# Batch 2's probabilities turned by a DMA crossing, batch 3's scores ahead of batch 2's packed product, slot 1's stores from GpSimd, packed keys turned at step 14

## The chip, the cores and the metric

The kernel runs on one core of one Trainium2 chip. The metric is the device time of one launch in microseconds, the median of several runs. Engines are named as in the profile: PE (TensorE, matrix products), PEld (its weight loads), ACT (ScalarE), DVE (VectorE), POOL (GpSimd) and SP (SyncE, which here only issues DMAs). PSUM, where PE writes, has eight banks.

## The reference, cut to what matters

```python
def sm_attn(qq, kk, vv):                       # softmax attention, scale 1/8
    a = softmax(scale * qq @ kk.T)
    return a @ vv
p_packed = sm_attn(p, k, v)                    # 32 packed queries per head
out = sm_attn(q, p_packed, p_packed)           # 576 queries read the packed result
x = out.transpose(0, 2, 1, 3).reshape(8 * 576, 512)
h = x @ w_in                                   # 512 -> 2048
return (h * cos(h)) @ w_out                    # 2048 -> 512
```

There are 8 batches, 8 heads, 576 positions and head size 64. All is given and returned in float32; the kernel computes its products in bfloat16.

## The kernel before, in words

Positions stand as p = 6·row + c, so that a batch is 96 rows of 6 columns. For each batch b the kernel does the following.

- **Loads.** GpSimd's queue loads k, q and v (`load`, line 94) and casts them to bfloat16 on the way. `behind(t)` (line 98) makes GpSimd wait for a tile before the loads that are written after it: batch 3's v and q and batch 4's k wait so until the turned q of batch 2 has landed.
- **Turning.** q and k are needed with the head's 64 values on the partitions. For batches 0 and 1, and for batch 2's keys, PE turns them (`pe_T`, line 116); from batch 3's keys and batch 2's queries on, SP issues a DMA that turns them on its way from SBUF to SBUF (`xbar`, line 102), called a crossing here.
- **First attention.** `s1` (line 143) makes the scores of the 32 packed queries against k, and ACT exponentiates them into `a1` (line 152). These probabilities are turned to `a1T`, for batches 0, 1 and 2 by PE and a copy on DVE (`a1_pe`, line 176), for the others by a crossing (`a1_xbar`, line 166). `pp` (line 186) multiplies `a1T` with v, and `pp_T` (line 198) turns the result into the packed keys `ppT`.
- **Second attention, folded into the first weights.** `ppw` (line 213) multiplies the packed result with w_in once per batch. `s2`, `sums2` and `normalise` (lines 231 to 249) give the normalised probabilities `a2n`.
- **Slot.** `slot` has 16 steps. Each multiplies `a2n` with 128 columns of the folded weights (`h_mm`, line 263: four products of 288 columns), ACT takes the cosine out of PSUM (line 267), and DVE multiplies both into `gT` (line 270).
- **Output.** `out_gen` (line 351) multiplies `gT` with w_out, 16 products of 512 columns per chunk of 128 rows. A chunk is copied out of PSUM to one of four `osb` tiles, by ACT inside a slot and by DVE between slots, and stored by SP (line 357).

The order on each engine is written out by hand. The output products are the filler: `fill(n)` puts n of them between other work, so that PE has something to do while ACT and DVE work. Inside a slot, `slot` spreads what is left, less `keep`, over the steps by weight. An entry fc: (weight, behind) in `heavy` gives a step more of them, and `behind` says how many of that step's come after the hooks (other work called at that step); a step without an entry has its hooks ahead of all of its filler. The call `last` places `pp_T` of the next batch between step 15's product and its DVE multiply.

PSUM is shared out, from slot 1 on, as two banks for the output products and three pairs of banks (pool `psA`) for all else. A new user of a pair waits on PE until the last reader of an earlier user has finished; within the steps that matter here the three pairs go round.

The order around the change, before: slot 1 (batch 1), then batch 2's scores, its two turning groups with filler around them, its packed product `pp(2)` and directly behind it the scores of batch 3, then `pp_T(2)`, `s2(2)` and so on, then slot 2. SP's queue in this part holds: four stores, the crossings of k of batch 3 and q of batch 2, six stores, the crossing of batch 3's `a1`, the crossings of q of batch 3 and k of batch 4.

Of the kernel before, what the change touches and what calls it, by code (L numbers as in the profile page):

```python
# [9 lines left out]
BF16 = mybir.dt.bfloat16  # L10
# [5 lines left out]
def kernel(  # L16
# [10 lines left out]
    nc = tc.nc  # L27
# [79 lines left out]
    def pe_T(n, b, engs=(V, V, V), groups=(0, 1, 2), own=None):  # L107
        if 0 in groups:
            xT[n, b] = att_pool.tile([128, H * 3, TP], BF16, name=n + "T", tag=n + "T", bufs=2 if n == "k" else 1)
        t = xT[n, b]  # L110
        flat = bf[n, b].rearrange("p h x -> p (h x)")
        for i in groups:
            ps = own(BF16) if own else psa(BF16)[:, 0, :]
            for j in range(8):
                o = 8 * i + j
                nc.tensor.transpose(ps[:, j * TP:(j + 1) * TP], flat[:, o * 128:(o + 1) * 128],  # L116
                                    ident[0:TP, 0:TP])
            to = t[:, 8 * i:8 * i + 8].rearrange("p a x -> p (a x)"), ps[:, 0:8 * TP]
            if engs[i] is None:
                return to  # L120
            copy(engs[i], *to)
# [36 lines left out]
    def recips(b):  # L158
        r1[b] = small.tile([128, 2], FP32, name="r1")
        rs1[b] = small.tile([128, 2], FP32, name="rs1")  # L160
        V.reciprocal(r1[b], sums1[b])
        V.tensor_scalar(out=rs1[b], in0=r1[b], scalar1=scale, scalar2=None, op0=ALU.mult)

    def a1_xbar(b):
        t = a1T[b] = att_pool.tile([128, 2, C, 128], BF16, name="a1T", tag="a1T")
        nc.sync.dma_start_transpose(out=t.rearrange("p a c x -> p (a c) x"),
                                    in_=a1[b % 2].rearrange("p a c x -> p (a c x)"))

    def a1_pe(b, ys=(0, 1), own=None):
        if 0 in ys:  # L170
            a1T[b] = att_pool.tile([128, 2, C, 128], BF16, name="a1T", tag="a1T")
        t = a1T[b]
        for y in ys:
            ps = own(BF16) if own else psa(BF16)[:, 0, :]
            for c in range(C):
                nc.tensor.transpose(ps[0:TP, c * 128:(c + 1) * 128], a1[b % 2][:, y, c, 0:TP], ident)
            copy(V, t[0:TP, y].rearrange("p c x -> p (c x)"), ps[0:TP, 0:C * 128])

    def pp(b, eng=V, own=None):

        ps = own() if own else psa()[:, 0, :]
        for y in range(2):
            for j in range(C):
                c = 2 * (j % 3) + j // 3
                for x in range(4):
                    nc.tensor.matmul(ps[32 * x:32 * x + 32, y * D:(y + 1) * D],  # L186
                                     a1T[b][0:TP, y, j, 32 * x:32 * x + 32],
                                     bf["v", b][:, 2 * x + y, c * D:(c + 1) * D],
                                     start=(j == 0), stop=(j == C - 1))
        t = pp_sb[b % 2].rearrange("p a d -> p (a d)")  # L190
        copy(eng, t[:, 0:2 * D], ps[:, 0:2 * D])
        copy(eng, t[:, 2 * D:3 * D], ps[:, 0:D])
# [63 lines left out]
    def h_mm(b, fc):  # L256
        if fc == 0:
            g_tile(b)
        ps = psa()
        spare[0] = ps[:, 1, HS:512]  # L260
        for y in range(2):
            for e in range(2):
                nc.tensor.matmul(ps[:, e, 0:HS], PPW[b][:, y, fc * 128:(fc + 1) * 128],  # L263
                                 a2n[b][:, y, e * HS:(e + 1) * HS], start=(y == 0), stop=(y == 1))
        cs = cos_pool.tile([128, S], BF16, name="cosT")
        csv = cs.rearrange("p (e x) -> p e x", e=2)
        ACT.activation(out=csv, in_=ps[:, :, 0:HS], func=AF.Sin, bias=PI_HALF)  # L267

        def rest():
            V.tensor_tensor(out=gT[b][:, fc, :].rearrange("p (e x) -> p e x", e=2),  # L270
                            in0=ps[:, :, 0:HS], in1=csv, op=ALU.mult)
            if fc % 8 == 7:
                j0 = (b % 2) * 64
                G.tensor_copy(out=joint[b // 2][:, fc - 7:fc + 1, j0:j0 + 64],  # L274
                              in_=gT[b][:, fc - 7:fc + 1, 512:576])
        return rest
# [33 lines left out]
                        in0=t.rearrange("p a (f x) -> p (a f) x", x=64),  # L310
                        in1=cs.rearrange("p a (f x) -> p (a f) x", x=64), op=ALU.mult)

    osb_eng = [V]

    def pieces_of(b, c):
        ob = out[b * S:(b + 1) * S, :].rearrange("(p c) d -> c p d", c=C)
# [26 lines left out]
    def out_gen(b):  # L343
        groups = [(0, 1), (2,), (3,)] if b == 0 else [(c,) for c in range(n_chunks(b))]
        for grp in groups:
            pss = {c: O.tile([128, DM], FP32, name="ot", tag="ot") for c in grp}
            for f0 in range(0, NFC, 4):
                for c in grp:
                    for fc in range(f0, f0 + 4):
                        w = joint[b // 2][:, fc, :] if c == 4 else gT[b][:, fc, c * 128:(c + 1) * 128]  # L350
                        nc.tensor.matmul(pss[c], w, w_out_bf[:, fc, :],  # L351
                                         start=(fc == 0), stop=(fc == NFC - 1))
                        if fc == NFC - 1:
                            osb = o_pool.tile([128, DM], FP32, name="osb")
                            copy(osb_eng[0], osb, pss[c])
                            for a, z, rows in pieces_of(b, c):
                                nc.sync.dma_start(out=rows, in_=osb[a:z, :])
                        yield

    filler = []  # L360
# [7 lines left out]
    def fill(n):  # L368
        while n > 0 and filler:
            next(filler[0][0])  # L370
            filler[0][1] -= 1
            if filler[0][1] == 0:
                filler.pop(0)
            n -= 1
# [98 lines left out]
    set_filler(0)  # L473
    s2(1)
    ppw(1, 0, V)
    fill(4)
    sums2(1, 0)
    fill(1)
    sums2(1, 1)
    rest_ppw, = ppw(1, 1, (V, V), later=True)  # L480
    fill(3)
    normalise(1)
    ACT.preload_act_table_set(SIN_SET)
    rest_ppw()
    fill(7)

    def slot(s, hooks, keep=0, heavy={}, last=None):


        left = to_do() - keep  # L490
        weight = [1 + heavy.get(fc, (0, 0))[0] for fc in range(NFC)]
        for fc in range(NFC):
            rest = h_mm(s, fc)
            if fc == NFC - 1 and last:
                last()
            rest()
            quota = (left * sum(weight[:fc + 1])) // sum(weight) - (left + keep - to_do())
            behind = min(quota, heavy[fc][1]) if fc in heavy else quota
            fill(quota - behind)
            while hooks and hooks[0][0] == fc:  # L500
                hooks.pop(0)[1]()
            fill(behind)
# [24 lines left out]
    def cross(n, b):  # L527
        return lambda: xbar(n, b)

    osb_eng[0] = ACT  # L530
    slot(1, [(2, lambda: pw2(1, 2, (ACT, V))), (4, lambda: h_rest(0)), (6, lambda: pack_p(2, 4)), (7, cross("k", 3)),
             (8, tk2), (9, cross("q", 2)), (10, lambda: pe_T("k", 2, (V, V, ACT), (2,)))], 4, {2: (1, 2), 4: (3, 5)})
    ACT.preload_act_table_set(EXP_SET)
    osb_eng[0] = V
    behind(xT["q", 2][0:1, 0, 0:1])
    load("v", 3)
    load("q", 3)
# [2 lines left out]
    set_filler(1)  # L540
    fill(4)
    s1(2)
    fill(7)
    a1_pe(2, (0,))
    fill(3)
    a1_pe(2, (1,))
    recips(2)
    fill(7)
    pp(2)
    s1(3)  # L550
    a1_xbar(3)
    fill(2)
    pp_T(2)
    recips(3)
    fill(4)
    s2(2)
    ppw(2, 0, V)
# [14 lines left out]
        load(n, b)  # L572
    fill(9)
    osb_eng[0] = ACT
    slot(2, [(7, lambda: tiled(2))], 10, {7: (5, 4)}, lambda: pp_T(3, V))

    for s in range(3, B):
        nxt = s + 1 < B
        ACT.preload_act_table_set(EXP_SET)
        osb_eng[0] = V  # L580
        set_filler(s - 1)
        fill(5)
        s2(s)
        ppw(s, 0, V)
        fill(8 if nxt else 9)
        if nxt:
            s1(s + 1)
            ppw(s, 1, V)
            a1_xbar(s + 1)
            xbar("q", s + 1)  # L590
            recips(s + 1)
            if s + 2 < B:
                xbar("k", s + 2)
                behind(xT["k", s + 2][0:1, 0, 0:1])
        else:
            for n in range(1, 4):
                ppw(s, n, V)
        fill(4 if nxt else 5)
        sums2(s, 0)
        fill(5)  # L600
        sums2(s, 1)
        normalise(s)
        ACT.preload_act_table_set(SIN_SET)
        fill(13)
        osb_eng[0] = ACT
        for n, b in (("v", s + 2), ("q", s + 2), ("k", s + 3)):
            if b < B:
                load(n, b)
        if nxt:
            slot(s, [(7, lambda: tiled(s))], 5 if s % 2 else 13, {7: (5, 4)}, lambda: pp_T(s + 1, V))  # L610
        else:
            slot(s, [], 5)
    set_filler(B - 1)
# [32 lines left out]
```

## Time and profile before

| what | value |
|---|---|
| median of 3 runs | 245.31 us (245.04 to 246.25) |
| the profiled execution | 245.1 us |
| its span | 243.3 us |
| granted TensorE clock | 0.997 of full speed |
| PE, DVE, ACT, POOL busy in the span | 96%, 67%, 68%, 15% |
| DMA moved | 37.37 MB, mean 154 GB/s |

The page gives busy time by engine, a row of 40 slices for each, the chain of work that ended last, and groups of equal instructions with their mean time. Between about 35 us and the tail at 236 us PE starts one product after the other almost without a pause, so this kernel is read from the timeline: which product starts when, and which of the starts comes later than the end of the one before it. Times in a timeline are in us from the start of the span; the first column is the start, the second the length of the merged group, and the matmul lengths overlap (one of 512 columns shows 0.38 us but the next starts 0.216 us after it: thirteen of them fill 71.50 to 74.30).

### The profile page before, as it was taken

What the parts mean: (1) busy time and instruction counts of PE and PEld (TensorE: products, weight loads), DVE (VectorE), ACT (ScalarE), POOL (GpSimd) and SP (SyncE); (2) the same over time, 40 slices, a digit from 0 to 9 for tenths busy, and PEclk for the clock granted to TensorE, in tenths of its full rate; (3) what the DMA queues carried; (4) which work ended last, traced back from release to release, by engine and by line L of the source; (5) the groups of instructions that cost most, each with busy time, mean ns of one, the idle gap of its engine ahead of it and who ended that gap; (6) DMA issues with size and microseconds to landing.
All of it is one profiled execution on the core that took longest, in us unless ns stands there. A gap on an engine that the chain in (4) does not pass through costs nothing.

```text
span 243.3 us, 5484 instructions
## 1 busy us (share of the span) xinstructions
PE 233.8 (96%) x2251; PEld 128.9 (53%) x2251; DVE 162.0 (67%) x256; ACT 166.1 (68%) x267; POOL 37.4 (15%) x60
## 2 busy tenths in 40 slices
PE   7789899999999999999999999999999999999994
PEld 3454354566446564556455654655455645665453
DVE  3259997787568795778758675868667878784001
ACT  2349999778478696868787687858796666773110
POOL 8432230210400041004100510030101010011000
PEclk9999999999999999999999999999999999999998
DMA  6999999999799999997999899999292111311133
GB/s 94 203 205 206 204 206 229 199 237 187 163 184 183 219 179 180 197 197 163 158 199 219 162 221 204 188 164 176 66 192 52 31 46 43 86 36 53 46 84 86
DMA packets 64377, 37.37 MB, mean 154 GB/s; under 512 B 36865, under 2 KB 59777, under 8 KB 64353
## 3 DMA queue, kind: packets, MB, share of 16 engines
q0 software_dynamic: 23152, 18.75, 51.0%
q1 hardware_dynamic: 40960, 18.16, 35.9%
q8 instruction: 17, 0.28, 0.4%
q10 hardware_dynamic: 240, 0.13, 0.2%
q14 instruction: 8, 0.06, 0.1%
HBM read 37.22 MB, written 9.44 MB: 192 GB/s over the span
## 4 chain that ended last, share of the span: by engine, by line
PE 82%; DVE 6%; ACT 1%; issue 1%; ACTq 0%
PE ot L351 50%; PE psA L263 22%; DVE gT L295 3%; PE psA L213 3%; PE psA L143 2%; PE psA L239 2%; PE ot L337 1%; PE psA L186 1%; DVE gT L270 1%; DVE PPW L87 1%; ACT cosT L267 1%; ACT cosT L294 0%; PE psA L116 0%; DVE qT L87 0%; PE psA L303 0%
## 5 line engine op out<-in xcount | busy, mean ns | idle before, releaser
L351 PE MATMUL ot<-w_out_bf,gT 128*128 128x512 bf16 x512 | 134.0, 379 | 0.0
L270 DVE TENSOR_TENSOR gT<-psA,cosT 128x576 bf16<-128x576 f32 x112 | 83.3, 757 | 21.0 <-ACT cosT L267 19.9
L267 ACT ACTIVATE cosT<-psA 128x576 bf16<-128x576 f32 x112 | 72.9, 652 | 24.9 <-PE psA L263 23.5
L263 PE MATMUL psA<-a2n,PPW 128*128 128x288 bf16 x448 | 73.3, 286 | 0.0
L351 PEld LDWEIGHTS <-gT 128*128 128x128 bf16 x512 | 48.2, 98 | 39.5 <-issue 4.2
L263 PEld LDWEIGHTS <-PPW 128*128 128x128 bf16 x448 | 43.8, 98 | 30.1 <-issue 0.4
L87 DVE CAST PPW<-psA 128x1024 bf16<-128x1024 f32 (+1 forms) x24 | 26.8, 1131 | 6.4 <-PE psA L213 6.2
L85 ACT COPY osb<-ot 128x512 f32<-128x512 f32 (+1 forms) x23 | 13.1, 569 | 16.2 <-PE ot L351 13.9
L87 DVE COPY osb<-ot 128x512 f32<-128x512 f32 (+2 forms) x15 | 9.7, 645 | 20.4 <-PE ot L337 17.2
L274 POOL COPY joint<-gT 128x512 bf16<-128x512 bf16 x14 | 8.6, 618 | 78.2 <-DVE gT L270 78.2
L249 DVE SCALAR_TENSOR_TENSOR a2n<-a2u,r,lns 128x576 bf16<-128x576 bf16 x16 | 12.4, 814 | 9.6 <-ACT lns L247 9.6
L152 ACT ACTIVATE a<-psA 128x576 bf16<-128x576 f32 x16 | 10.2, 646 | 8.2 <-PE psA L143 8.2
L241 ACT ACTIVATE lns<-psA 128x576 f32<-128x576 f32 x16 | 10.3, 650 | 7.2 <-PE psA L239 6.7
L351 PE MATMUL ot<-w_out_bf,joint 128*128 128x512 bf16 x48 | 12.2, 380 | 0.0
L98 POOL COPY gate<-kT 1x1 bf16<-1x1 bf16 x4 | 0.7, 180 | 72.7 <-DMA kT<-kbf 72.7
L231 ACT ACTIVATE a2u<-psA,rs 128x576 bf16<-128x576 f32 x16 | 11.0, 737 | 1.1 <-PE psA L143 1.0
L247 ACT ACTIVATE lns<-lns 128x576 f32<-128x576 f32 x16 | 10.0, 673 | 0.0
L213 PE MATMUL psA<-w_in_bf,ppT 64*32 64x512 bf16 x224 | 9.8, 379 | 0.0
L295 DVE TENSOR_TENSOR gT<-psH,cosT 128x512 bf16<-128x512 f32 x15 | 9.3, 680 | 0.4 <-ACT cosT L294 0.4
L391 PE MATMUL ot<-wz 128*128 128x512 f32 (+2 forms) x13 | 7.5, 661 | 1.9 <-DVE wz L404 1.7
L294 ACT ACTIVATE cosT<-psH 128x512 bf16<-128x512 f32 x15 | 8.4, 628 | 0.7 <-DVE gT L295 0.4
L289 PE MATMUL psH<-a2n,PPW 128*128 128x512 bf16 x30 | 7.8, 381 | 0.8 <-DVE PPW L87 0.8
(88 smaller groups left out, 170.6 us busy)
## 6 DMA issues: line engine op xcount, KB each, us to landing
kbf<-in_k_dram POOLq DMA_DIRECT2D x8, 576.0 KB, 14.0
vbf<-in_v_dram POOLq DMA_DIRECT2D x8, 576.0 KB, 7.8
qbf<-in_q_dram POOLq DMA_DIRECT2D x8, 576.0 KB, 10.9
out_dram<-osb SPq DMA_DIRECT2D x24, 192.0 KB, 2.6
out_dram<-osb SPq DMA_DIRECT2D x22, 128.0 KB, 2.9
w_in_bf<-in_moe_w_in_dram POOLq DMA_DIRECT2D x4, 512.0 KB, 17.3
w_out_bf<-in_moe_w_out_dram POOLq DMA_DIRECT2D x4, 512.0 KB, 20.8
out_dram<-osb SPq DMA_DIRECT2D x25, 64.0 KB, 2.3
```

What stands on the lines that cost most here:

```text
L85: ACT.copy(out=out, in_=in_)
L87: eng.tensor_copy(out=out, in_=in_)
L152: ACT.activation(out=a1[b % 2][:, y, :, 0:TP].rearrange("p (e m) x -> p e m x", e=2), in_=ps[y][:, :, 0:HS].rearrange("p e (m x) -> p e m ...
L213: nc.tensor.matmul(ps[y][32 * x:32 * x + 32, :], ppT[b % 2][r, 0, x, :], w_in_bf[r, x, n * 512:(n + 1) * 512], start=True, stop=True)
L231: ACT.activation(out=a2u[b][:, y].rearrange("p (e x) -> p e x", e=2), in_=ps[y][:, :, 0:HS], func=AF.Exp, scale=rs1[b][:, y:y + 1])
L241: ACT.activation(out=lns[b][:, y].rearrange("p (e x) -> p e x", e=2), in_=ps[:, :, 0:HS], func=AF.Ln)
L249: V.scalar_tensor_tensor(out=a2n[b][:, y], in0=a2u[b][:, y], scalar=r1[b][:, y:y + 1], in1=lns[b][:, y], op0=ALU.mult, op1=ALU.mult)
L263: nc.tensor.matmul(ps[:, e, 0:HS], PPW[b][:, y, fc * 128:(fc + 1) * 128], a2n[b][:, y, e * HS:(e + 1) * HS], start=(y == 0), stop=(y == 1))
L267: ACT.activation(out=csv, in_=ps[:, :, 0:HS], func=AF.Sin, bias=PI_HALF)
L270: V.tensor_tensor(out=gT[b][:, fc, :].rearrange("p (e x) -> p e x", e=2), in0=ps[:, :, 0:HS], in1=csv, op=ALU.mult)
L295: return lambda: V.tensor_tensor(out=gT[b][:, fc, 0:512], in0=ps, in1=cs, op=ALU.mult)
L351: nc.tensor.matmul(pss[c], w, w_out_bf[:, fc, :], start=(fc == 0), stop=(fc == NFC - 1))
```

## The change

Batch 2's probabilities are turned by a crossing on SP in place of twelve PE transposes and two DVE copies. Batch 3's scores, with its own crossing, move ahead of batch 2's packed product. `a1T` gets a second buffer. In slot 1 the stores are issued by GpSimd. The next batch's packed keys are turned by PE after the filler of step 14, ahead of step 15's product, in slots 2 to 6. The filler is shared out anew: one more ahead of slot 1, seven fewer in it (38 for 45), nine more between slots 1 and 2, three fewer in slot 2 (27 for 30). The lines from 166 on move by a few: line 263 before is line 264 after, line 351 is 352.

```diff
+    def a1_tile(b):
+        a1T[b] = att_pool.tile([128, 2, C, 128], BF16, name="a1T", tag="a1T", bufs=2)
+        return a1T[b]
+
     def a1_xbar(b):
-        t = a1T[b] = att_pool.tile([128, 2, C, 128], BF16, name="a1T", tag="a1T")
-        nc.sync.dma_start_transpose(out=t.rearrange("p a c x -> p (a c) x"),
+        nc.sync.dma_start_transpose(out=a1_tile(b).rearrange("p a c x -> p (a c) x"),
                                     in_=a1[b % 2].rearrange("p a c x -> p (a c x)"))
...
-    osb_eng = [V]
+    osb_eng, store = [V], [nc.sync]
...
-                                nc.sync.dma_start(out=rows, in_=osb[a:z, :])
+                                store[0].dma_start(out=rows, in_=osb[a:z, :])
...
     s2(1)
     ppw(1, 0, V)
-    fill(4)
+    fill(5)
     sums2(1, 0)
     fill(1)
     sums2(1, 1)
     rest_ppw, = ppw(1, 1, (V, V), later=True)
-    fill(3)
+    fill(2)
     normalise(1)
     ACT.preload_act_table_set(SIN_SET)
     rest_ppw()
-    fill(7)
-
-    def slot(s, hooks, keep=0, heavy={}, last=None):
+    fill(8)
+
+    def slot(s, hooks, keep=0, heavy={}):
...
         for fc in range(NFC):
-            rest = h_mm(s, fc)
-            if fc == NFC - 1 and last:
-                last()
-            rest()
+            h_mm(s, fc)()
...
-    osb_eng[0] = ACT
+    osb_eng[0], store[0] = ACT, G
     slot(1, [(2, lambda: pw2(1, 2, (ACT, V))), (4, lambda: h_rest(0)), (6, lambda: pack_p(2, 4)), (7, cross("k", 3)),
-             (8, tk2), (9, cross("q", 2)), (10, lambda: pe_T("k", 2, (V, V, ACT), (2,)))], 4, {2: (1, 2), 4: (3, 5)})
+             (8, tk2), (9, cross("q", 2)), (10, lambda: pe_T("k", 2, (V, V, ACT), (2,)))], 10, {2: (1, 2), 4: (3, 5)})
     ACT.preload_act_table_set(EXP_SET)
-    osb_eng[0] = V
+    osb_eng[0], store[0] = V, nc.sync
     behind(xT["q", 2][0:1, 0, 0:1])
...
     set_filler(1)
     fill(4)
     s1(2)
-    fill(7)
-    a1_pe(2, (0,))
-    fill(3)
-    a1_pe(2, (1,))
-    recips(2)
-    fill(7)
-    pp(2)
+    a1_xbar(2)
+    fill(9)
     s1(3)
     a1_xbar(3)
-    fill(2)
+    recips(2)
+    recips(3)
+    fill(16)
+    pp(2)
+    fill(3)
     pp_T(2)
-    recips(3)
     fill(4)
     s2(2)
...
-    slot(2, [(7, lambda: tiled(2))], 10, {7: (5, 4)}, lambda: pp_T(3, V))
+    slot(2, [(7, lambda: tiled(2)), (14, lambda: pp_T(3, V))], 10, {7: (5, 4), 14: (0, 0)})
...
-            slot(s, [(7, lambda: tiled(s))], 5 if s % 2 else 13, {7: (5, 4)}, lambda: pp_T(s + 1, V))
+            slot(s, [(7, lambda: tiled(s)), (14, lambda: pp_T(s + 1, V))], 5 if s % 2 else 13,
+                 {7: (5, 4), 14: (0, 0)})
```

(`a1_pe` loses its argument `ys` and takes its tile from `a1_tile`; batches 0 and 1 still use it as before.)

More of the change, by code (lines that the diff above doesn't have):

```diff
@@ L162, in recips, with a1_pe @@
         V.tensor_scalar(out=rs1[b], in0=r1[b], scalar1=scale, scalar2=None, op0=ALU.mult)
+    def a1_tile(b):
+        a1T[b] = att_pool.tile([128, 2, C, 128], BF16, name="a1T", tag="a1T", bufs=2)
+        return a1T[b]
     def a1_xbar(b):
-        t = a1T[b] = att_pool.tile([128, 2, C, 128], BF16, name="a1T", tag="a1T")
-        nc.sync.dma_start_transpose(out=t.rearrange("p a c x -> p (a c) x"),
+        nc.sync.dma_start_transpose(out=a1_tile(b).rearrange("p a c x -> p (a c) x"),
                                     in_=a1[b % 2].rearrange("p a c x -> p (a c x)"))
[L169 to L173, printed above, removed]
+    def a1_pe(b, own=None):
+        t = a1_tile(b)
+        for y in range(2):
             ps = own(BF16) if own else psa(BF16)[:, 0, :]
```

## Prediction

> **What bounds the kernel now.** First the page: busy time, the slices, the chain that ended last.
>
> ```profile
> PE 233.8 (96%) x2251; PEld 128.9 (53%) x2251; DVE 162.0 (67%) x256; ACT 166.1 (68%) x267; POOL 37.4 (15%) x60
> ...
> PE   7789899999999999999999999999999999999994
> ...
> PE 82%; DVE 6%; ACT 1%; issue 1%; ACTq 0%
> ```
>
> PE is full from the seventh slice to the last but one and is 82% of the chain. Whatever shortens or stops PE there moves the end by as much; work taken off DVE or ACT does not. So I read the timeline for PE's order and for the few places where a product starts late. First the stretch behind slot 1:
>
> ```profile
> 61.91 0.44 PE L143 MATMUL psA<-kT,P 64*32 64x288 bf16 x16
> ...
> 62.28 1.69 PE L351 MATMUL ot<-w_out_bf,gT 128*128 128x512 bf16 x7
> 63.80 0.50 PE L176 MATMUL psA<-ident,a 128*96 128x128 bf16 x6
> 64.14 0.81 PE L351 MATMUL ot<-w_out_bf,gT 128*128 128x512 bf16 x3
> 64.78 0.50 PE L176 MATMUL psA<-ident,a 128*96 128x128 bf16 x6
> 65.12 1.67 PE L351 MATMUL ot<-w_out_bf,gT 128*128 128x512 bf16 x7
> 66.72 0.55 PE L186 MATMUL psA<-vbf,a1T 96*32 96x64 bf16 x48
> 67.21 0.44 PE L143 MATMUL psA<-kT,P 64*32 64x288 bf16 x16
> ```
>
> Starts follow each other without a pause: an output product (F below) takes 0.216, a turning group 63.80 to 64.14 = 0.34, scores 0.37, the packed product 0.49, and entering scores or packed product from F costs 0.09 (7 F from 65.12 would end at 66.63, line 186 starts at 66.72). Then the end of slot 3, steps 13 to 15, where `pp_T` stands:
>
> ```profile
> 113.46 0.65 PE L263 MATMUL psA<-a2n,PPW 128*128 128x288 bf16 x4
> ...
> 114.15 1.36 ACT L267 ACTIVATE cosT<-psA 128x576 bf16<-128x576 f32 x2 [0.27 <-PE psA L263]
> ...
> 114.84 1.46 DVE L270 TENSOR_TENSOR gT<-psA,cosT 128x576 bf16<-128x576 f32 x2 [0.16 <-ACT cosT L267]
> ...
> 115.65 0.27 PE L198 MATMUL psA<-ident,pp_sb 128*128 128x128 bf16 x2
> ```
>
> This shows how long a pair of PSUM banks is held. Step 13's product starts at 113.46 and takes 0.49; its cosine starts 0.20 later, its DVE multiply at 114.84 (0.76 long, to 115.60), and the transposes of `pp_T`, the next user of that pair, start at 115.65: **2.19 us from product to reuse**, with nobody idle in between. `pp_T` came 0.07 late for it (step 15's product ends at 115.58). With three pairs, the third allocation after a product starts 2.19 after it at the earliest.
>
> **The change, part by part** (us; plus is slower).
>
> 1. *Turning by PE gone.* Two groups of 0.34: **-0.68**. The two DVE copies (0.55 each) lie beside PE's work: 0.
>
> 2. *Batch 3's scores alone.* They followed the packed product directly; now they are entered from F: **+0.09**. Their keys landed at 60.9 (crossing issued 51.10, 9.8 to landing) and are needed at about 63.4.
>
> 3. *Ahead of slot 1.* The second sum of exponentials waits 0.17 for ACT (F ends at 37.22, line 239 starts at 37.39); the added F fills that. But the logarithms run 0.17 later, and the second half of step 0's product, which waits 0.20 for `a2n`, waits 0.37. **0**.
>
> 4. *Slot 1 with 38 F for 45.* Steps shrink to 0.49 + 2 F = 0.92 or less, so PE meets held pairs sooner. Step 3 would come at 44.24, but step 2's pair is held until 42.23 + 2.18 = 44.41: 0.17. Step 7 waits 0.08 now, because line 309 (1.23 on DVE) pushes step 5's multiply; with one F less ahead of it, 0.30. With 0.05 of small ones: **+0.4** (bounds 0 and 7 F = 1.5).
>
> 5. *The crossing.* It replaces work that waits for nothing by a round trip. Batch 2's last exponential ends 3.53 us after step 15's product (60.30 to 63.83; the table load sets it). Now `pp(2)` stands after 6 F, scores, 9 F, scores, 16 F: 31 x 0.216 + 2 x 0.37 + 3 x 0.09 = 7.7 after that product. The crossing has 7.7 - 3.5 = **4.2 us**. Its five rows:
>
> ```profile
> L166 SPq DMA_TRANSPOSE a1T<-a x5: 1484/3791/4300, 69.0 to 174.6; - x5
> ...
> DMA to landing us min/median/max: 3.9/8.3/12.0
> ```
>
> Asked one by one: 12.0 at 69.0, 10.2 at 95.6, 8.3 at 121.6, each with loads of v, q, k in flight; 4.4 at 148.7, where the last load was just landing; 3.9 at 174.6 with none. So the bounds of the wait are 0 and 12.0 - 4.2 = 7.8. Here it would be issued at about 63.1 on SP, where the crossings of k and q ahead of it are through by 61.8; GpSimd lets the next loads go when q has landed, now 64.71, first load issued at 65.00. So it starts ahead of the loads and ends among them. I take 5.8, nearer to the quiet rows: **+1.6**. PE has nothing else queued that could pass it: all F, `pp_T(2)` and `s2(2)` stand behind.
> The Trainium skill, "DMA: Bandwidth & Descriptors", gives DMA transposes 261 GB/s (Latency and other measured facts) and a fixed 2.0 us per DMA (Anatomy of one DMA): estimated from them, 0.39 MB is 3.5 us, no wait, and the sum would be 1.6 smaller. The 3.9 row comes near that; the 8.3 to 12.0 rows differ, and they decide.
>
> 6. *Stores by GpSimd.* Six issues of some 0.8 (its loads' rows: 0.77) on an engine 15% busy; behind them stand the `joint` copies and the gate, and their sources come later anyhow. SP gains little: batch 3's k crossing starts at 51.10, when k lands (50.99: issued 30.67, 20.3 to landing). The stores queue behind the load of v (lands at 59.3). An `osb` is wanted again at about 67. **0**; if they held up q, term 5 carries it.
>
> 7. *Slot 2 with 27 F for 30.* Steps 0 to 2 have one F each: 3 x (0.49 + 0.216) = 2.12, under 2.19: 0.07. `pp(3)` writes into step 7's pair: PE comes to it 0.49 + 3 F + 0.09 + 0.56 (line 213) = 1.79 after that product, and waits 0.40, where now it waits 0.25. An `osb` copy (0.58 on ACT) then falls into step 3: 0.1. **+0.3** (bounds 0 and 3 F = 0.65).
>
> 8. *`pp_T` at step 14.* It does the same 0.11 of work, but takes the pair that step 15's product had; that product now takes step 13's, held for 2.19. PE reaches it 0.49 + F of step 13 + 0.49 + F of step 14 + 0.11 after step 13's product. By the slot's formula those F are 1 and 1 in slot 2, 1 and 2 in slot 3, 2 and 2 in slots 4 to 6: 1.53, 1.74, 1.95, so it waits 0.66, 0.45 and 3 x 0.24. The old waits go: 0.14 in slot 2 (line 198 at 89.72, product ends at 89.58), 0.07 in slot 3, none after. 0.52 + 0.38 + 0.72 = **+1.6** (bounds 0 and 1.8, no old wait returned). Nothing covers it: filler of step 14 is already spent. `s2` gets its pairs a little sooner, but it waits for none now (line 143 at 117.36, F end at 117.27, and 0.09 is the entry).
>
> Sum: -0.68 + 0.09 + 0 + 0.4 + 1.6 + 0.3 + 1.6 = **+3.3**. On the profiled execution's 245.1 that is 248.4; it stands 0.2 below the median of the runs, so **248.6**.
>
> **The rivals.**
>
> *The crossing starves.* If the loads start before it, it lands with them, as in the rows of 8.3 to 12.0: wait 4.1 to 7.8 instead of 1.6, so 251 to 255. For: its issue and the first load's are within 2 us. Against: it stands behind q's crossing on SP, whose landing releases the loads. The Trainium skill, "TensorE: Matmul & The Clock Gate" (Why this matters for your kernels), warns that after a PE pause of over about 3 us the clock halves for a while. No pause of that length after the start is in this trace, so no number here rests on it.
>
> *The crossing is in time.* Landing in 4.2 as at 148.7: term 5 is 0, 247.0.
>
> *Not slower: step 15 finds its pair free.* Place: the third pair in slots 2 to 6. If `pp_T` at step 14 costs no wait, terms 8 (1.6) and most of 5 must go: a pair freed within 1.53 to 1.95 of its product rather than 2.19 is the point from which it decides; then, with the crossing at 4.4 (wait 0.2), 245.3 - 0.59 + 0.7 + 0.2 = 245.6. Against: 2.19 is a chain of three engines, none idle in it.
>
> *Faster.* Only terms 1 and 2 gain, 0.59, or 244.7; over 0.5% needs twice that.
>
> **How the numbers follow.** The forecast, 247.3 to 250.5, 0.58; starved 0.15; in time 0.14; not slower 0.10; faster 0.03. The range runs from 246.0 (terms 1, 2 and 8 alone give 246.3, and 0.3 for the measurement) to 253.0 (a wait of 6). A measurement here can tell 0.5%, 1.23 us, from no change: faster 0.03; same 0.12, with a little of the in-time case; slower 0.85.
>
> **What would show it.** Right: in slots 2 to 6 the product of step 15 starts 2.19 after that of step 13; line 187's first packed product behind the 16 F waits for `a1T`'s crossing; the turning groups at 63.8 and 64.8 are gone. Wrong: no gap ahead of step 15; the crossing landing within 4.2; or q of batch 2 landing much after 65, which would delay `s2(2)` and all loads.

## The result and the profile after

| | before | after |
|---|---|---|
| median | 245.28 us (245.04 to 246.25, 7 runs) | 247.29 us (246.91 to 250.67, 7 runs) |
| the profiled execution | 245.1 | 247.9 |
| its span | 243.3 | 246.1 |
| granted TensorE clock in it | 0.997 | 1.0 |

The ratio is 1.0087, with an interval of 1.0059 to 1.0115: slower by 0.6 to 1.2%. The run of 250.67, the only one with a granted clock below 0.997 (0.992), is not in the ratio. The forecast was 248.6, slower: 1.3 too high. The median stands at the lower edge of the forecast's own band, 247.3 to 250.5.

From the page of the kernel after: busy time, PE's row of slices, the chain that ended last.

```profile
PE 235.2 (96%) x2239; PEld 128.3 (52%) x2239; DVE 161.1 (65%) x254; ACT 166.5 (68%) x267; POOL 40.5 (16%) x66
...
PE   7889899999999999999999999999999999999994
...
PE 69%; DMA 22%; DVE 3%; ACT 3%; issue 1%; POOL 1%; ACTq 0%; POOLq 0%
```

Busy shares and slices look as before, though 2.8 us were lost: the losses are pauses of tenths. What changed visibly is the chain: DMA holds 22% of it, where it was not named among the first five before. Short waits of PE for a transfer pull the whole life of that transfer into the chain. The share does not say what they cost, only where to look.

PE's timeline behind slot 1, in the same execution (start, length, group, and in brackets the idle time before it and what ended that):

```profile
61.18 0.44 PE L143 MATMUL psA<-kT,P 64*32 64x288 bf16 x16
61.55 2.12 PE L352 MATMUL ot<-w_out_bf,gT 128*128 128x512 bf16 x9
64.00 0.44 PE L143 MATMUL psA<-kT,P 64*32 64x288 bf16 x16 [0.34 <-DMA kT<-kbf]
64.37 3.63 PE L352 MATMUL ot<-w_out_bf,gT 128*128 128x512 bf16 x16
67.93 0.56 PE L187 MATMUL psA<-vbf,a1T 96*32 96x64 bf16 x48
68.42 0.82 PE L352 MATMUL ot<-w_out_bf,gT 128*128 128x512 bf16 x3
69.07 0.28 PE L199 MATMUL psA<-ident,pp_sb 128*128 128x128 bf16 x2
```

The two turning groups are gone, and `pp(2)` at 67.93 waits for nothing: the crossing was there. What waits is the scores of batch 3 (64.00), for keys whose own crossing had been issued at 52.24 and landed at 63.96. The crossings of probabilities in this stretch, by the tile's view (durations in ns, then landing times in us):

```profile
L169 SPq DMA_TRANSPOSE a1T<-a x2: 1492/3512/5532, 64.0 to 67.0; - x2
...
DMA to landing us min/median/max: 3.8/9.7/15.7
```

Batch 2's, issued at 64.01 ahead of the loads (first one at 66.31), took 3.8; batch 3's, issued at 66.96 among them, took 15.7. Batch 2's could have gone out at 63.32, when its last exponential ended; SP was busy with the crossing of q until 63.96. Now the end of slot 4, as an example for slots 2 to 6:

```profile
142.00 0.65 PE L264 MATMUL psA<-a2n,PPW 128*128 128x288 bf16 x4
...
142.92 0.65 PE L264 MATMUL psA<-a2n,PPW 128*128 128x288 bf16 x4
...
143.84 0.27 PE L199 MATMUL psA<-ident,pp_sb 128*128 128x128 bf16 x2
144.18 0.65 PE L264 MATMUL psA<-a2n,PPW 128*128 128x288 bf16 x4
```

Steps 13, 14, the packed keys, step 15. The packed keys take 0.11, so PE is free at 143.95; step 15 starts at 144.18, which is 2.18 after step 13. That is the held pair of the prediction, to the hundredth.

**Where the time went.** For each stretch between two landmarks of PE, after less before, with the output products that were moved into or out of it taken out at 0.216 each. The second column of measured values is a later profiled execution of the same kernel after (247.69 us), from the experiments below. F is one output product, as in the prediction.

| stretch (landmarks are first products) | F moved | predicted | first | second |
|---|---|---|---|---|
| start to slot 1 | +1 | 0 | +0.23 | +0.18 |
| slot 1, to batch 2's scores | -7 | +0.4 | +0.33 | +0.19 |
| batch 2's scores to `s2(2)` | +9 | +1.0 | -0.16 | +0.26 |
| `s2(2)` to `s2(3)`, slot 2 | -3 | +0.82 | +0.96 | +0.96 |
| `s2(3)` to `s2(4)`, slot 3 | 0 | +0.38 | +0.81 | +0.38 |
| slots 4 to 6 | 0 | +0.72 | +0.69 | +0.68 |
| sum | 0 | +3.3 | +2.86 | +2.65 |

The two executions are 0.6 and 0.2 above the medians of their runs (247.29 and 247.51), so of the sums some 2.0 to 2.3 is what a usual run loses. What is behind slot 6 is unchanged within 0.06. The 0.81 of slot 3 holds a wait that the second execution doesn't have:

```profile
109.72 0.56 PE L187 MATMUL psA<-vbf,a1T 96*32 96x64 bf16 x48 [0.36 <-DMA a1T<-a]
```

Batch 4's crossing was issued at 97.00 and landed at 109.68; before, it landed at 105.88. And the start holds a wait for a load that both kernels issue alike (in the second execution it is 0.22):

```profile
38.95 1.89 PE L352 MATMUL ot<-w_out_bf,gT 128*128 128x512 bf16 x8 [0.30 <-DMA w_out_bf<-in_moe_w_out_dram]
```

This is scatter rather than the change: counted the same way, the stretch is -0.25 to +0.31 in the seven other profiles that have the start of after and ran it at full clock (e1, e2, e5, e7, e8, e9 and e12 of the experiments below), and +0.14 to +0.43 in the three that have the start of before (e4, e6 and e10).

### The profile page after: what moved, and what is told of

Read it like the earlier page. It is cut to its first block, busy times and chain, and to the rows that moved or that the text cites. A ratio compares the mean times of both kernels' runs of the same rounds, so it can differ in the third digit from the quotient of the medians.

```text
span 246.1 us, 5464 instructions
## 1 busy us (share of the span) xinstructions
PE 235.2 (96%) x2239; PEld 128.3 (52%) x2239; DVE 161.1 (65%) x254; ACT 166.5 (68%) x267; POOL 40.5 (16%) x66
## 4 chain that ended last, share of the span: by engine, by line
PE 69%; DMA 22%; DVE 3%; ACT 3%; issue 1%; POOL 1%; ACTq 0%; POOLq 0%
PE ot L352 41%; PE psA L264 18%; DMA w_out_bf<-in_moe_w_out_dram 9%; DMA a1T<-a 5%; DMA kT<-kbf 5%; DMA kbf<-in_k_dram 3%; DVE gT L271 2%; PE psA L214 2%; PE psA L143 2%; ACT cosT L268 2%; PE psA L187 1%; PE ot L338 1%; PE psA L240 1%; PE psA L116 1%; ACT a L152 1%
## 5 line engine op out<-in xcount | busy, mean ns | idle before, releaser
L85 ACT COPY osb<-ot 128x512 f32<-128x512 f32 (+1 forms) x23 | 13.1, 568 | 16.2 <-PE ot L352 13.9
L392 PE MATMUL ot<-wz 128*128 128x512 f32 (+2 forms) x13 | 8.1, 715 | 1.9 <-DVE wz L405 1.7
```

The costliest lines, as they stand in the source:

```text
L85: ACT.copy(out=out, in_=in_)
```

## The experiments

The theory going in: the loss is the held pair at step 15 (some 1.5 us) with the thinner slots 1 and 2 (some 0.9); the crossing costs little because it starts ahead of the loads. The rival: the crossing, or the DMA traffic that the change rearranges, is the larger part. A measured ratio is to the kernel before, measured beside it on the same chip. The kernel before had there 245.07 us for experiments 1, 2, 3 and 6, 245.22 for 4, 5, 7 and 11, 245.18 for 8, 9 and 10, and 245.11 for 12.

**1. Packed keys at the old place, the rest as after** (e1_old_keys).

```diff
-    slot(2, [(7, lambda: tiled(2)), (14, lambda: pp_T(3, V))], 10, {7: (5, 4), 14: (0, 0)})
+    slot(2, [(7, lambda: tiled(2))], 10, {7: (5, 4)}, lambda: pp_T(3, V))
```

and the same in slots 3 to 6.

> The changed kernel with the packed keys turned at their old place, between step 15's product and its DVE multiply. Theory (term 8: step 15's product waits for step 13's pair of PSUM banks): the waits of 0.55, 0.45 and 3 x 0.23 us ahead of step 15 in slots 2 to 6 go and 0.14 and 0.07 ahead of the turning come back, so some 1.5 us less than the changed kernel: about 245.8 (245.4 to 246.4), ratio to the kernel before 1.000 to 1.005. Rival (the loss is DMA's alone, the keys' place costs nothing): unchanged at about 247.3, ratio 1.008.

246.28 us (245.54 to 247.6), ratio 1.0049 [1.0027, 1.0072]: 1.0 below after, where 1.5 was expected, and at the upper end of the expected range; the rival's 247.3 falls. The runs scatter over 2 us, and the profiled one (247.6) is the longest. Its timeline says what ate the gain there:

```profile
93.56 0.81 PE L352 MATMUL ot<-w_out_bf,gT 128*128 128x512 bf16 x3
96.42 0.44 PE L143 MATMUL psA<-kT,P 64*32 64x288 bf16 x16 [2.05 <-DMA P<-p_bf]
```

PE comes to batch 4's scores before the packed queries have crossed (issued 90.57, behind the crossing of batch 4's keys on SP, landed 96.37). In that execution the 1.5 were saved and more than that was lost again to the DMA queue. The direction holds; the size had to be measured elsewhere, by experiment 2.

**2. Packed keys at step 14 alone, in the kernel before** (e4_keys_alone).

```diff
-    slot(2, [(7, lambda: tiled(2))], 10, {7: (5, 4)}, lambda: pp_T(3, V))
+    slot(2, [(7, lambda: tiled(2)), (14, lambda: pp_T(3, V))], 10, {7: (5, 4), 14: (0, 0)})
```

and the same in slots 3 to 6.

> The kernel before with one part of the change alone: the packed keys turned after step 14's output products. Theory (term 8): step 15's product waits until 2.19 after step 13's; with 2 and 1 output products there in slot 2 that is +0.31, then +0.38 and 3 x 0.24: 1.4 us, about 246.7, ratio 1.005 to 1.007. Rival (a wait moved, not added): 245.3, ratio 1.000.

246.58 us (246.37 to 246.81), ratio 1.0057 [1.0045, 1.0069]: +1.5 us, against a term of +1.6. Step 14, the keys and step 15 at the end of slot 2 (step 13 started at 87.61):

```profile
88.53 0.65 PE L263 MATMUL psA<-a2n,PPW 128*128 128x288 bf16 x4
...
89.23 0.28 PE L198 MATMUL psA<-ident,pp_sb 128*128 128x128 bf16 x2
89.86 0.65 PE L263 MATMUL psA<-a2n,PPW 128*128 128x288 bf16 x4 [0.35 <-DVE gT L270]
```

Step 15 waits for DVE's multiply, the last reader of step 13's pair, and starts 2.25 after step 13 (2.18 or 2.19 in slots 3 to 6). The rival, that a moved product finds its pair free, falls.

**3. Slot 1's stores back on SP, the rest as after** (e2_sp_stores).

```diff
-    osb_eng[0], store[0] = ACT, G
+    osb_eng[0], store[0] = ACT, nc.sync
```

> The changed kernel with slot 1's stores on SP again. Theory (GpSimd's stores save nothing, and what made batch 3's scores wait 0.42 us for the k crossing was a late load): 247.0 to 248.0; the k crossing again starts when k lands, but the crossing of batch 2's probabilities is issued up to 1 us later, behind two more stores on SP, and the packed product may wait 0.3 to 1.5 for it. Rival (the stores in GpSimd's queue hold up the crossings of k and q, and so the loads behind the gate): 0.8 us faster than the changed kernel, about 246.4, with k of batch 3 turned by 61.

Six runs: 247.77, 247.82, 251.84, 253.27, 253.52 and 255.03; the four long ones had granted clocks of 0.984 to 0.990. The profiled run is one of the two short ones:

```profile
63.57 3.63 PE L352 MATMUL ot<-w_out_bf,gT 128*128 128x512 bf16 x16
68.29 0.56 PE L187 MATMUL psA<-vbf,a1T 96*32 96x64 bf16 x48 [1.09 <-DMA a1T<-a]
```

Two stores on SP (62.22 and 62.85) push the crossing to 64.31, 1.38 after the last exponential ended (62.93); it still takes 3.93, but only 1.06 is left between its issue and the first load's (65.37), and `pp(2)` waits 1.09. So stores on SP make the crossing late; that GpSimd's stores are what keeps the kernel after from such long runs is not shown, since no profile has one. Experiment 5 shows a way to such times.

**4. Stores by GpSimd alone, in the kernel before** (e6_stores_alone).

```diff
-    osb_eng[0] = ACT
+    osb_eng[0], store[0] = ACT, G
```

with `store` brought in and switched back to SP behind slot 1, as in the change.

> The kernel before, with the stores of slot 1 issued by GpSimd in place of SP, and nothing else. Theory: they cost nothing and gain nothing by themselves, since no load or crossing of slot 1 waits for them: 245.1 to 245.4, ratio 0.999 to 1.002. Rival: the issues on GpSimd delay the gate behind which the next loads stand, or q's crossing gets ahead on SP, by half a microsecond or more: outside of that range.

244.97 us (244.71 to 246.04), ratio 0.9992 [0.9983, 1.0002]: nothing by themselves, as the prediction's term 6 had it; the ratio is inside the expected one. The profiled execution (246.04) is the longest of the twelve: there `pp(3)` in slot 2 waits 1.02 for batch 3's crossing, landed at 83.17 (80.99 in the profile of before).

**5. The loads ahead of the crossing** (e5_no_gate).

```diff
     osb_eng[0], store[0] = V, nc.sync
-    behind(xT["q", 2][0:1, 0, 0:1])
     load("v", 3)
```

> The kernel after, with the loads of batch 3's v and q and batch 4's k no longer gated on batch 2's q: they are issued about 4 us earlier, at some 62, ahead of the crossing of batch 2's probabilities (issued at 64.01 in the kernel after, landed 3.77 later). Theory: what decides the crossing is whether loads are under way when it starts; among them it takes the 8 to 12 us that the crossings of later batches take, lands at 72 to 76, the packed product at 67.93 waits 4 to 8 us, and the time is 251 to 255. Rival: the crossing takes under 4.5 us wherever it stands: the time stays at 247.3, within 0.5.

260.71 us (255.53 to 261.51). Of the three loads only that of v comes earlier, at 61.91 (q's follows at 67.43). The crossing is issued at 63.22 and lands 10.61 later; q's own crossing is under way for 3.6 of it, about as long as in experiments 7 and 12 (3.4), where it took 4.52. The timeline of the profiled execution (255.53), and the same stretch in windows (the last three columns are granted clock, DMA share, GB/s):

```profile
63.83 3.63 PE L352 MATMUL ot<-w_out_bf,gT 128*128 128x512 bf16 x16
73.87 0.83 PE L187 MATMUL psA<-vbf,a1T 96*32 96x64 bf16 x48 [6.41 <-DMA a1T<-a]
```

```profile
60.00:68.00 8.00, 7.30 (x62) 2.86 (x60) 3.09 (x8) 4.53 (x10) 1.92 (x3) 1.00 1.13 176
68.00:72.00 4.00, 0.00 (x0) 0.00 (x0) 0.00 (x0) 0.00 (x0) 0.98 (x2) 0.97 1.27 117
72.00:78.00 6.00, 3.80 (x64) 1.83 (x73) 0.71 (x3) 0.00 (x0) 0.00 (x0) 0.50 1.29 207
78.00:80.00 2.00, 2.00 (x31) 0.76 (x30) 1.04 (x1) 1.46 (x3) 0.00 (x0) 0.86 1.28 190
```

Two costs, one behind the other: PE stands 6.41, and then works at half clock up to 78.6, 4.7 us after it resumed, which loses another 2.3. Together 8.7, close to 255.53 less 247.3. The other three runs, 5 us longer again, have a clock of 0.971 to 0.973 where this one has 0.984: half clock for about 0.028 x 2 x 259 = 14.5 us instead of 0.016 x 2 x 254 = 8.1, of which 6.8 lie in these windows (71.74 to 78.56). This is the starved crossing of the prediction, made on purpose, and its price is higher than the 251 to 255 given there and here. In the profiled execution it is the clock that takes it beyond (without the 2.3 it would be 253.2); for the three longer runs that is worked out from their mean clocks alone. The Trainium skill, "TensorE: Matmul & The Clock Gate" (Why this matters for your kernels), warns of idle gaps over about 3 us; this gap of 6.41 agrees, and the waits of 1.09 and 2.05 above left the clock at 0.999 and 1.0. The threshold itself is not measured here. The Trainium skill, "DMA: Bandwidth & Descriptors" (Queues, rings and completion order), has each DMA engine alternate packet by packet between the queues that hold work; a crossing that takes 10.6 behind one load and 3.8 ahead of it fits that, but no run here shows the packets' order.

**6. Batch 2's probabilities turned by PE, the rest as after** (e3_pe_turn).

```diff
-    a1_xbar(2)
...
-    fill(16)
+    fill(6)
+    a1_pe(2)
+    fill(10)
```

> The changed kernel with batch 2's probabilities turned by PE again (two groups after the sixth of the 16 output products), all else as changed. Theory from the changed kernel's trace (the crossing landed 0.06 us ahead of need and cost nothing): 0.6 us slower than the changed kernel in an execution like that, about 247.9. Rival (term 5 as predicted: in most executions the packed product waits 1 to 2 us for the crossing): 0.4 to 1.4 us faster, 246.0 to 247.0, and with less spread between runs.

The profiled execution (253.57) ran at a clock of 0.95 throughout. The other three are 247.23, 247.34 and 247.71, ratio 1.0092 [1.0076, 1.0108]: the same as after, neither the theory's 247.9 nor the rival's 246.0 to 247.0. So in the kernel after, crossing and turning by PE cost alike. If turning costs its 0.68 here too (no undisturbed profile shows it), the crossing with what comes with it takes back about that much, between the theory (nothing) and the prediction's 1.6.

**7. Batch 3's scores back behind the packed product, the rest as after** (e7_scores_back).

```diff
-    fill(9)
-    s1(3)
-    a1_xbar(3)
     recips(2)
-    recips(3)
-    fill(16)
+    fill(27)
     pp(2)
-    fill(3)
+    s1(3)
+    a1_xbar(3)
+    fill(1)
     pp_T(2)
+    recips(3)
```

> The kernel after, with batch 3's scores and the crossing of its probabilities back behind batch 2's packed product (27 output products ahead of the packed product, none between its parts). Theory: batch 3's crossing is issued 2 us later, at about 69, does not start beside the first loads, and these land within 15.5 to 16 us of their first issue instead of 19.2; so the wait of 0.43 for batch 4's crossing and that of 0.34 for batch 3's keys go, and 0.09 of entering: 246.4 to 246.8. Rival: the loads are slow because batch 2's probabilities cross as well, or by chance: 247.3, with landings at 19 us.

247.67 us (247.5 to 248.1), ratio 1.0104 [1.0088, 1.0120]. The expectation failed. In its profile the landings did come nearly as expected (16.2 us after the first issue, no wait for batch 4's crossing), but two other waits took their place: 0.36 for batch 2's crossing, and 0.71 at `pp(3)` for batch 3's, now issued at 69.98 and landed at 83.22. Taking one transfer out of the way of others puts it in its own consumer's way.

**8. Batch 3's scores ahead, alone, in the kernel before** (e10_scores_alone).

```diff
     a1_pe(2, (0,))
-    fill(3)
+    fill(1)
+    s1(3)
+    a1_xbar(3)
+    fill(2)
     a1_pe(2, (1,))
     recips(2)
-    fill(7)
+    recips(3)
+    fill(6)
     pp(2)
-    s1(3)
-    a1_xbar(3)
-    fill(2)
+    fill(3)
     pp_T(2)
-    recips(3)
```

and two buffers for `a1T`.

> The kernel before with batch 3's scores and the crossing of its probabilities ahead of batch 2's packed product (and a second buffer for the crossed probabilities, which that order needs); batch 2's are turned by PE as before. Theory: the crossing is issued some 2 us earlier, ahead of the load of k, and all loads that start beside it land later: k lands 17 to 17.7 us after its issue, where it lands 14 to 15.3 where the scores stand behind; the time moves by 0.1 of entering and 0 to 0.6 of waits for later crossings: 245.3 to 245.9. Rival: the late landings came from batch 2's crossing: k lands within 15.3, 245.2 to 245.3.

245.33 us (245.01 to 245.88), ratio 0.9997 [0.9981, 1.0013], and the load of k lands 14.16 after its issue, though the crossing was issued at 66.66, ahead of it (67.22). The time lies at the edge of both ranges; the landing decides. The theory that the early crossing by itself delays the loads falls. That the two crossings together do is not tested by this run, which has one of them.

**9. The kernel after once more** (e11_after_again), unchanged.

> The kernel after once more, unchanged, on the same chip as the two others: 246.9 to 247.4, ratio 1.007 to 1.009. It says whether e7_scores_back, whose 247.5 to 248.1 were measured in another call, is slower than it (then the early scores gain more by the packed product of batch 3 than they lose by the loads) or the same.

247.51 us (247.01 to 247.89), ratio 1.0080 [1.0050, 1.0110], 0.1 above the expected range. So e7 is not faster than it, and the early scores are worth nothing that these intervals resolve. The profile is a second sample of the crossing:

```profile
63.41 0.44 PE L143 MATMUL psA<-kT,P 64*32 64x288 bf16 x16
63.78 3.63 PE L352 MATMUL ot<-w_out_bf,gT 128*128 128x512 bf16 x16
68.11 0.56 PE L187 MATMUL psA<-vbf,a1T 96*32 96x64 bf16 x48 [0.71 <-DMA a1T<-a]
```

The scores of batch 3 did not wait here, so PE came to `pp(2)` at 67.4; the crossing was issued at 63.16, as its last exponential ended (63.14), and took 4.91: a wait of 0.71. In the first execution the wait of 0.34 for the keys had given the crossing its time, though it was issued 0.85 later. Here batch 3's crossing, issued at 66.64, took 7.53 where it had taken 15.67, the load of k landed 13.95 after its issue, not 17.58, and batch 4's crossing made nobody wait.

**10. Both moves back, the crossing and the counts kept** (e9_both_back): experiment 7 with the packed keys of experiment 1.

> The kernel after with two things undone: the packed keys at the old place, and batch 3's scores behind batch 2's packed product. Left of the change are the crossing of batch 2's probabilities, the stores by GpSimd, and slot 1 with 38 and slot 2 with 27 output products within them. It differs from the kernel of 244.6 us (e8_best) only by these counts. Theory, by the prediction's sizes (0.4 for slot 1, less the 0.2 that 41 products still cost; 0.3 for slot 2; up to 0.4 where the packed product of batch 3 meets its crossing): 245.1 to 245.6. Rival: the counts cost much more than predicted, as the 1.0 us would say by which e7_scores_back less the 1.5 us of the packed keys stands above the predicted sum: 246.0 to 246.4.

246.12 us (245.39 to 247.43), ratio 1.0030 [1.0007, 1.0053]. That is in the rival's range: the counts cost more than I had sized; experiment 12 says where. (The counts differ from e8_best's in slots 3 to 5 as well, see experiment 11, which the expectation leaves out.) With experiments 1, 7 and 9 it makes a square. Scores ahead: 247.51 with the keys at step 14, 246.28 with them at the old place. Scores behind: 247.67 and 246.12. By these medians the keys' place is worth 1.2 and 1.6, and the scores' place 0.2 with either sign. The four were not measured side by side and each ratio's interval reaches 0.4 to 0.7 us to either side, so the first is clear and the second can't be told from nothing.

**11. What is left as gain** (e8_best): the crossing and GpSimd's stores; the keys at the old place, the scores behind; 41 output products in slot 1, 55 between the slots (after has 53), 28 of them between batch 2's scores and `pp(2)`, 30 in slot 2, and, to make up for these, 31, 34 and 35 in slots 3, 4 and 5 where both other kernels have 34, 37 and 37.

```diff
-             (8, tk2), (9, cross("q", 2)), (10, lambda: pe_T("k", 2, (V, V, ACT), (2,)))], 10, {2: (1, 2), 4: (3, 5)})
+             (8, tk2), (9, cross("q", 2)), (10, lambda: pe_T("k", 2, (V, V, ACT), (2,)))], 7, {2: (1, 2), 4: (3, 5)})
...
-    slot(2, [(7, lambda: tiled(2)), (14, lambda: pp_T(3, V))], 10, {7: (5, 4), 14: (0, 0)})
+    slot(2, [(7, lambda: tiled(2))], 2, {7: (5, 4)}, lambda: pp_T(3, V))
...
+            slot(s, [(7, lambda: tiled(s))], {3: 0, 4: 11, 5: 5, 6: 13}[s], {7: (5, 4)}, lambda: pp_T(s + 1, V))
```

(The order between the slots is that of experiment 7, with `fill(28)` and `fill(2)`.)

> What the runs so far leave as gain, without what they show as cost: the crossing of batch 2's probabilities and the stores by GpSimd are kept; the packed keys are turned at the old place, batch 3's scores stand behind the packed product, slot 1 keeps 41 output products within it for 38, slot 2 has 30 as before. Theory: the two turning groups are gone (-0.68 us), slot 1 costs some 0.2, the crossing 0 to 0.3: 244.6 to 245.0 against 245.1 of the kernel before. Rival: the crossing costs more than its 3.8 us in most executions: 245.5 or more.

244.58 us (244.28 to 244.75), ratio 0.9968 [0.9952, 0.9984]: faster than both kernels, by 0.2 to 0.5% against before. The crossing, issued at 63.05, took 3.77, and no landing made PE wait in this stretch:

```profile
61.69 5.99 PE L352 MATMUL ot<-w_out_bf,gT 128*128 128x512 bf16 x27 [0.16 <-issue]
67.61 0.56 PE L187 MATMUL psA<-vbf,a1T 96*32 96x64 bf16 x48
```

(The 28th product's record is missing; its 0.2 shows as idle.) With the moved products taken out, the stretch from batch 2's scores to `s2(2)` is 0.67 shorter than before: the two turning groups of term 1, with nothing taken back in this execution.

**12. The same with 38 in slot 1** (e12_slot1_38), the three then falling into slot 2.

```diff
-             (8, tk2), (9, cross("q", 2)), (10, lambda: pe_T("k", 2, (V, V, ACT), (2,)))], 7, {2: (1, 2), 4: (3, 5)})
+             (8, tk2), (9, cross("q", 2)), (10, lambda: pe_T("k", 2, (V, V, ACT), (2,)))], 10, {2: (1, 2), 4: (3, 5)})
```

> The kernel of e8_best with slot 1 at 38 output products instead of 41, as in the kernel after; the three then fall into slot 2, which has 33. It tells where the 1.5 us lie that e9_both_back takes more than e8_best, with 38 in slot 1, 30 for 32 between the slots and 27 in slot 2. Theory: not in slot 1's held banks, which cost 0.2 for these three as predicted, but in PE coming to batch 3's packed product ahead of its crossing (0.98 us of wait in e9's profile); here it comes there as late as in e8_best and waits for nothing: 244.6 to 244.9, ratio 0.997 to 0.999. Rival: slot 1 with 38 costs 1 us or more: 245.6 or more.

244.97 us (244.45 to 245.59), ratio 0.9993 [0.9982, 1.0005]. That is just above the theory's range and far from the rival's: of the 1.5 us between e8 and e9 some 0.4 are these three products in slot 1. The profiles say where the rest is (less before, moved products taken out):

| stretch | e8 | e12 | e9 |
|---|---|---|---|
| start to slot 1 | -0.13 | +0.31 | -0.03 |
| slot 1 | -0.04 | +0.26 | +0.20 |
| batch 2's scores to `s2(2)` | -0.67 | -0.45 | -0.63 |
| slot 2 | -0.14 | -0.31 | +1.23 |
| slots 3 to 6 | +0.24 | +0.24 | 0.00 |

Slot 1 is 0.30 longer with three products fewer. The rest is slot 2, and most of it the wait at `pp(3)`:

```profile
81.31 0.63 PE L214 MATMUL psA<-w_in_bf,ppT 64*32 64x512 bf16 x16
82.92 0.56 PE L187 MATMUL psA<-vbf,a1T 96*32 96x64 bf16 x48 [0.98 <-DMA a1T<-a]
```

Two output products fewer ahead of slot 2 and three fewer in it bring PE earlier to a crossing that lands when it lands (issued 69.36, landed 82.87). In e12 the same product starts at 83.53, behind a landing at 82.59, without a wait. The fewer products in slots 3 to 5 cost e8 and e12 0.24; a kernel without that was not run.

## Why the prediction was right, and where not

- **Right in sign and main cause.** Term 8 carries it: +1.6 predicted, +1.5 alone (experiment 2), 1.2 to 1.6 within the change (1, 7, 9, 10). Its working holds slot by slot: 0.38 predicted and measured in slot 3 of the second execution, 0.72 against 0.69 and 0.68 in slots 4 to 6, and 2.18 from step 13 to step 15 where 2.19 was read from before. The turning groups are gone, as foretold. Of its signs of being wrong two came nevertheless: the crossing landed within 4.2 in the first execution (3.77), and q of batch 2 landed at 66.02 and 66.94 instead of 64.71, which moved the loads but made `s2(2)` wait for nothing.
- **Term 5, the crossing, was mis-sized.** The step that failed is "So it starts ahead of the loads and ends among them. I take 5.8". The place was right in the second execution: issued at 63.16 (63.1 predicted; 64.01 in the first), the budget of 4.2 as worked out, and in both the loads did start before it landed, by 1.5 and 0.8. But it took 3.77 and 4.91 in the two executions, 3.77 to 4.52 in six other kernels that issue it ahead of the loads (e1, e2, e7, e8, e9 and e12), and never 5.8. Wait: 0 and 0.71 instead of 1.6; experiment 6 puts the crossing at about 0.6. Issued one to four microseconds ahead of the loads, it kept about the speed of the quiet rows; the middle between the rows stood for nothing that happens here. What its length does go with, in these eight profiles, is how long q's own crossing is still under way: 3.77 to 3.93 where that landed 0.8 to 2.6 after the issue, 4.23 at 2.9, 4.52 at 3.4 (twice), 4.91 at 3.8. It does not go with the time beside the loads (0.8 at 4.91, 2.9 at 3.93). No run varies this alone. The prediction counted q's crossing as through on SP and as the gate of the loads, but not as company; SP was through with it at 63.96 and 62.12, not 61.8. The rival with 247.0, the crossing in time, was nearer in this term than the forecast. So was the 3.5 us that term 5 estimates from the Trainium skill, though the fixed 2.0 us in it is given there for DMAs that GpSimd issues, and SP issues this one.
- **Luck.** The first execution's +2.86 against +3.3 looks closer than the working was: 0.42 at batch 3's scores and 0.43 in slot 3, both put at nothing, stand in for part of the 1.6 that the crossing didn't cost.
- **Terms 1 and 2** (-0.68, +0.09) are in the third row of the table: -0.16 is their -0.59 and 0.42 at the scores of batch 3, and +0.26 is -0.59, 0.71 and 0.14 not placed.
- **Term 2 took for granted** that the keys, landed at 60.9 before, would be there at 63.4. In the first execution they landed at 63.96, in the second at 61.23. In the first both parts had moved: the load of k landed at 52.15 for 50.99, and the crossing took 11.71 for 9.78. The margin of 2.5 us was less than that.
- **Terms 4 and 7.** Slot 1: +0.33 and +0.19 for +0.4. Slot 2 with term 8's part: +0.96 both times for +0.82. With the scores behind, slot 2 costs more, 0.4 in experiment 7 (+1.35 for +0.96) and 0.9 over the predicted 0.3 in experiment 10 (+1.23), by a wait that the prediction's way of counting, PSUM pairs alone, could not show. In the change itself batch 3's crossing is issued earlier, and in neither execution does `pp(3)` wait for it.
- **Term 3** (0): +0.23 and +0.18 were measured at the start, both times with a wait for a load of w_out, but the start scatters by more than this between executions, so neither is put down to the change.
- **Term 6** (0): right alone (experiment 4). But together with the crossing the stores matter (experiment 3), which the prediction mentioned only in passing, as SP's gain being little.
- **The starved crossing** was priced at 251 to 255 without the clock. Made to happen, it is 255.5 to 261.5.

**What stays open.** Why the same loads landed 17.6 us after issue in one execution of the kernel after and 13.95 in another, and 13.6 to 15.3 in eight profiles of kernels with one crossing less or later (before, e4, e6, e7, e8, e9, e10, e12). My explanation, that batch 3's early crossing stands in their way, fell in this form with experiments 8 and 9. A narrower one is left: with both crossings in front, batch 3's took 15.0 to 15.7 and the load of k 17.0 to 17.7 where batch 3's was issued 0.6 to 2.0 behind the first load (after, e1, e2), and 7.53 and 13.95 where it was issued 0.6 ahead of it (e11). Four profiles are no test of it. Nor was a long run of experiment 3 seen in a profile; that it starves as in experiment 5 is argued from the clocks alone.

## What to carry to other kernels

When a group of products is put between two users of a ring of PSUM pairs, count the chain from product to last reader (here 2.18 us), and how much work PE has in between: what is missing is lost once per slot, and the profile of before holds all the numbers for it. A DMA that stands in for PE work is decided by what is under way when it starts, so let the bulk loads start behind it, keep its queue free of stores, and leave it as much filler as the longest time seen when it goes ahead of the loads (here 4.91, for 3.77 at best). Filler taken out ahead of a landing saves nothing, since PE then waits there instead; check each later landing before spending its margin.

## What the runs showed of the hardware

- The same 0.39 MB crossing takes 3.77 to 4.91 us when issued 1.1 to 4.1 us ahead of three casting loads (eight profiles), and 10.61 when issued 1.3 us behind one of them (one profile).
- In e5, PE paused from 67.46 to 73.87 (6.41 us); half clock was granted from 71.74 on, 4.3 us after the last product's end, and full clock came back at 78.6, 4.7 us after the first product of the next burst. A pause of 2.05 us (e1) left it at 1.0.
- Landing times of one and the same program scatter by microseconds between executions (keys of batch 3: 63.96 and 61.23; load of k: 13.95 and 17.58 after issue), while PE's own stretches repeat to 0.01 or 0.02 (slots 4 to 6: 0.69 and 0.68 over before).
